# Partial sums of y added up in DRAM by accumulating transfers instead of on the vector engine

## The chip, the cores and the metric

One core of a Trainium2 chip runs the kernel. The metric is the device time of one execution in microseconds (us). Five engines work side by side, each with its own instruction stream: TensorE (PE, matrix products; PEld is its weight load), VectorE (DVE), ScalarE (ACT), GpSimd (POOL) and SyncE (SP). Transfers between DRAM and the on-chip memory SBUF are issued by an engine's stream and carried by 16 DMA engines that all streams share. PE writes only to PSUM, eight banks of 128 x 512 floats.

## What is computed

```
x = retention(q, k, v)                 # 4 x 576 = 2304 tokens, 512 wide
h = x @ w_in;  g = h * tanh(softplus(h));  x2 = g @ w_out      # first layer, d_ff 2048
h = max(x2 @ w_in2, 0);  out = (h * h) @ w_out2                # second layer, d_ff 2048
```

The retention part takes the first 63 us of the span and is not touched by the change's text. All matrices of the two layers are split into a high and a low part (fp32r), and each product is made of three matmuls.

## The kernel before

**Staging.** Tokens are cut into three blocks of SB = 768 (index v). The 2048 inner columns are cut into four quarters (index p, a pass). A *visit* u is one (layer m, pass p, block v), in the order m, p, v: 24 visits, numbered 0 to 23, of some 31 us each. Visits 0 to 11 are the first layer, visits 12 to 23 the second. Each visit has two half-visits, `fp` 0 and 1; each makes seven products (P1 to P7, a Strassen-like scheme on the block, L735) from the seven tiles `ring` (the split x of the block) and the weights `win`.

**The second product.** `y_group` (L812) multiplies the activated g with `wout` and collects y in four PSUM tiles `py`, over the four f of a visit. The y of visit u is made partly in visit u and finished in visit u+1: in the first layer, token half th = 0 is finished by y03 and th = 1 by y13, at the end of the first half-visit; in the second layer both are finished at the end of the visit's second half (names `y00` to `y13` in the lists `first_half`, `second_half`, `run`).

**Adding up.** y of the first quarter (p = 0) is copied by ACT from `py` into the tile `part[v]` (SBUF). y of quarters 1 to 3 is added onto it by DVE (L836). After the last quarter, `part` of the first layer is x of the second: `sums_x` and `split_x` form the seven sums and split them into `ring`. In the second layer the last quarter's sum is stored to `out` by SP, 19 transfers (the last block of 128 tokens in two halves of 256 columns).

**x again.** ring of a block is kept in DRAM (`keep`, tile `d`) at its first visit and fetched (`fetch`, seven transfers of 768 KB) for each later one, into the same seven tiles as PE frees them. For visit 3 alone x is loaded unsplit from the DRAM copy `raws` and split again (`again_x`).

**Order.** A class `Plan` records every operation with a cost, works out due times backwards from PE's fixed order, and then lists the operations per engine by due time. So an operation that is added or taken away can move others, far from where it stands; the order on each engine and on SP's and POOL's queues is then fixed, and each stream waits in order. The lines that the change and the prediction touch: `dma` (L288, SP's transfers), `y_group` (L812, L836), `again_x` and `load`, `scale_v` (L494 on ACT, L496 on POOL and DVE), `update` (the state copies `sbd`, L274 is the common ACT helper).

```
            if p == 0:
                act(dst, y, n=n, reads=[("py", o)], writes=kd)
            else:
                dve(
                    lambda dst=dst, y=y: nc.vector.tensor_tensor(dst, y(), dst, op=ALU.add),
                    n, [("py", o)] + kd, kd,
                )
```

Of the kernel before, what the change touches and what calls it, by code (L numbers as in the profile page):

```python
# [8 lines left out]
F32 = mybir.dt.float32  # L9
# [3 lines left out]
ALU = mybir.AluOpType  # L13
# [6 lines left out]
DM = H * D  # L20
DFF = 2048
P = 128
KD = DM // P
# [6 lines left out]
NPASS = NF // FPP  # L30
TH = 384
SB = 2 * TH
NSB = NT // SB
# [2 lines left out]
GS = 12  # L36
ES = 4
CPS = 4
WARM = 8
OUT_SLOTS = 6  # L40
PAD = 96
# [18 lines left out]
SLACK = 3.0  # L60
# [167 lines left out]
def kernel(  # L228
# [25 lines left out]
    cst = space("cst", **att_kw)  # L254


    part = tiles_of(act_p, NSB, [P, KD, SB], F32, "part")
    part2 = [t.rearrange("p k n -> p (k n)").rearrange("p (t e) -> p t e", e=DM) for t in part]
# [7 lines left out]
    py = tiles_of(ps_p, 4, [P, DM], F32, "py")  # L266
    t2 = act_p.tile([P, 2, TH], F32, tag="t2", name="t2")
    t3 = act_p.tile([P, 2, TH], F32, tag="t3", name="t3")

    plan = Plan()  # L270
    late = {}

    def act(out, in_, func=AF.Copy, n=512, reads=(), writes=(), **kw):
        fn = lambda: nc.scalar.activation(out() if callable(out) else out, in_() if callable(in_) else in_, func, **kw)  # L274
        plan.add("ACT", 0.09 + n * 0.00084, fn, reads, writes)

    def dve(fn, n, reads, writes):
        plan.add("DVE", 0.07 + n * 0.00104, fn, reads, writes)
# [8 lines left out]
    def dma(out, in_, reads, writes, size, early=0.0, slack=0.0, by=1e9, eng=None, cost=0.45):  # L287
        fn = lambda: (eng or nc.sync).dma_start(out=out, in_=in_)  # L288
        plan.add("SP", cost, fn, reads, writes, size / 0.40e6, early=early, slack=slack, by=by)

    def minus(eng, out, a, b):
        return lambda: eng.tensor_tensor(out, a, b.bitcast(F32), op=ALU.subtract)  # L292
# [38 lines left out]
    def split_in(gp):  # L331
# [26 lines left out]
            cut(2, slice(2, 4), yb, kb, 512)  # L358
        return lambda: cut(2, slice(2, 3), a21, kb, 256)

    raws = [dram_p.tile([P, 2, TH], F32, tag=f"raw{i}", name="xraw") for i in range(4)]
# [5 lines left out]
    def load(dst, i, kd, early=0.0):  # L367
        dma(dst, raws[i], [("raws", i)], [kd], P * 8 * TH, early=early)

    def first_x(i):  # L370
        b, ks = blocks_of(0)
        cut_x(i, b[(0, 1, 3, 2)[i]], ks[(0, 1, 3, 2)[i]])

    def again_x(name):
        i = X_AT[name]
        lo = [r[:, 1].bitcast(F32) for r in ring]
        kl = [("x", i, 1) for i in range(7)]
        tt = nc.vector.tensor_tensor
        t1 = sums.rearrange("p a n -> p (a n)").rearrange("p (k n) -> p k n", k=2)
        k1 = [("s", j) for j in range(3)]  # L380
        if name == "P1":
            load(t2, 0, "t2", 10.0)
        if name in ("P1", "P2", "P3"):
            load(lo[i], i if i < 2 else 3, kl[i], 4.0)
            cut_x(i, lo[i], kl[i])
        elif name == "P6":
            load(lo[4], 3, kl[4], 4.0)
        elif name == "P5":
            load(lo[3], 2, kl[3], 4.0)
            dve(lambda: tt(t3, lo[4], lo[3], op=ALU.subtract), 768, [kl[4], kl[3]], ["t3"])  # L390
            dve(lambda: tt(t1, lo[3], t2, op=ALU.subtract), 768, [kl[3], "t2"], k1)
            dve(lambda: tt(t2, lo[4], t1, op=ALU.subtract), 768, [kl[4], *k1], ["t2"])
            cut_x(4, t2, "t2")
            cut_x(3, t1, *k1)
        elif name == "P7":
            cut_x(5, t3, "t3")
        elif name == "P4":
            load(lo[6], 1, kl[6], 4.0)
# [260 lines left out]
    done_with += [("cp", j) for j in range(CPS)] + [("e", j) for j in range(ES)]  # L659
    plan.loose.add(plan.add("PE", 0.0, open_late, (), done_with))  # L660

    visits = [(m, p, v) for m in range(2) for p in range(NPASS) for v in range(NSB)]
    nv = len(visits)
    count = dict(g=0, e=0, ac=0, py=0, cp=0, direct=0)
    gs = {}

    def take(what, n):
        count[what] += 1
        return (count[what] - 1) % n
# [118 lines left out]
    def y_group(u, th, f):  # L788
        m, p, v = visits[u]
        g = m * NF + p * FPP + f  # L790
        j = gs.pop((u, th, f))
        kw = ("wo", g % OUT_SLOTS)
        na = KD if m == 0 else TH // P
        last = (u, th) == (nv - 1, 1)
        if f == 0:
            yb[0] = [take("py", 4) for _ in range(na + last)]
            yc = [slice(0, DM)] * na
            if last:
                yc[-1:] = [slice(0, DM // 2), slice(DM // 2, DM)]
            yb[1] = yc  # L800
        for i, (o, cols) in enumerate(zip(*(yb[k] for k in range(2)))):
            ky = ("py", o)

            def mm(i=min(i, na - 1), o=o, cols=cols):
                s = slice(i * P, i * P + P)
                y, gt, wo = py[o], late["g"][j], late["wout"][g % OUT_SLOTS]
                if m == 0:
                    y, st, mv = y[:, :TH], wo[:, :, s], gt
                else:
                    y, st, mv = y[:, cols], gt[:, :, s], wo[:, :, cols]  # L810
                for k, (a, b) in enumerate(((1, 0), (0, 1), (0, 0))):
                    nc.tensor.matmul(  # L812
                        y, st[:, a], mv[:, b],
                        start=(f == 0 and k == 0), stop=(f == FPP - 1 and k == 2),
                        skip_group_check=True,
                    )

            plan.add("PE", 0.52 if m == 0 else 0.694 * (cols.stop - cols.start) / DM, mm, [kw + (0,), kw + (1,), ("g", j, 0), ("g", j, 1), ky], [ky])
        if f < FPP - 1:
            return  # L820
        for i, (o, cols) in enumerate(zip(yb[0], yb[1])):
            i = min(i, na - 1)
            if m == 0:
                dst, n = part[v][:, i, TH * th : TH * th + TH], TH
                kd = [("part", v, i // 2, th)]
            else:
                dst, n = part2[v][:, 3 * th + i, cols], cols.stop - cols.start
                kd = [("p2", v, 3 * th + i, cols.start)]
                if p == 0:
                    kd += [("part", v, k, t) for k in range(2) for t in range(2)]  # L830
            y = lambda o=o, c=slice(0, TH) if m == 0 else cols: py[o][:, c]
            if p == 0:
                act(dst, y, n=n, reads=[("py", o)], writes=kd)
            else:
                dve(
                    lambda dst=dst, y=y: nc.vector.tensor_tensor(dst, y(), dst, op=ALU.add),  # L836
                    n, [("py", o)] + kd, kd,
                )
            if m == 1 and p == NPASS - 1:
                r = SB * v + TH * th + P * i  # L840
                dma(out[r : r + P, cols], dst, kd, [("out", r, cols.start)], P * 4 * n)

    first_half = "P1 P2 y03 P6 P5 y10 P7 y11 P4 y12 P3 y13".split()
    second_half = "P1 P2 y00 P6 P5 P7 y01 P4 y02 P3".split()
# [153 lines left out]
```

## Time and profile before

| | |
|---|---|
| time, median of 3 runs | 819.7 us (819.58 to 819.82) |
| the profiled execution's own time | 819.48 us |
| its span, first to last instruction | 817.7 us |
| PE busy | 810.6 us, 99% |
| DVE / ACT / POOL busy | 577.5 / 446.2 / 11.5 us |
| DMA traffic | 188.78 MB, 62.0% of the 16 engines' time |
| granted TensorE clock | 1.000 |

The profile gives busy time per engine, the chain of work that ended last (followed back from the last instruction), waits by releaser, and the transfers with the time from issue to landing. PE's busy time is that of pipelined matmuls; where they follow each other without a gap, PE sets the pace.

### The profile page before, as it was taken

The numbers are of one execution on the slowest core, as the hardware profiler recorded it, in microseconds if no ns is written. First come the engines' busy times: TensorE is split into PE (matmuls) and PEld (weight loads), VectorE is DVE, ScalarE is ACT, GpSimd is POOL, SyncE is SP. The second block draws the span as 40 slices with busy tenths as digits, with TensorE's granted clock in tenths as the row PEclk, the third lists the DMA queues.
The fourth block names the chain that finished last, engine by engine and source line by source line (L and its number), as shares of the span: only waits on it lengthen the run. The fifth ranks groups of instructions, "written<-read, shape, count | busy, mean of one in ns | idle before, by whom it ended". The sixth has DMA issues, their size and how long they took to land.

```text
span 817.7 us, 13326 instructions
## 1 busy us (share of the span) xinstructions
PE 810.6 (99%) x5216; PEld 770.3 (94%) x5216; DVE 577.5 (71%) x1096; ACT 446.2 (55%) x916; POOL 11.5 (1%) x20
## 2 busy tenths in 40 slices
PE   9999999999999999999999999999999999999998
PEld 7899999999999999999999898898898898898996
DVE  5899997987488636785489984995479844743443
ACT  2697586753455335553377675763465553652541
POOL 3200000000000000000000000000000000000000
PEclk9999999999999999999999999999999999999999
DMA  9985865984675754763844844963756843735812
GB/s 342 405 307 183 319 262 201 387 304 173 246 249 190 282 203 128 313 224 152 290 174 177 322 179 168 346 235 140 270 186 218 343 155 116 270 135 213 303 44 78
DMA packets 44158, 188.78 MB, mean 231 GB/s; under 512 B 4928, under 2 KB 6848, under 8 KB 44096
## 3 DMA queue, kind: packets, MB, share of 16 engines
q1 hardware_dynamic: 44096, 187.93, 62.0%
q8 instruction: 41, 0.67, 0.3%
q14 instruction: 21, 0.17, 0.1%
HBM read 148.59 MB, written 39.32 MB: 230 GB/s over the span
## 4 chain that ended last, share of the span: by engine, by line
PE 95%; DMA 4%; ACT 0%; DVE 0%; SPq 0%; issue 0%; DVEq 0%; ACTq 0%
PE py L812 48%; PE h L735 41%; PE h L773 2%; DMA qk<-in_qk_dram 1%; PE h L517 1%; DMA kv<-in_v_t_dram 1%; PE py L571 1%; DMA kv<-in_kv_dram 1%; PE py L535 1%; PE py L549 1%; DVE part L836 0%; ACT sbd L274 0%; ACT kv L494 0%; SPq L288 0%; DVEq L993 0%
## 5 line engine op out<-in xcount | busy, mean ns | idle before, releaser
L735 PE MATMUL h<-ring,win 128*128 128x384 f32 x1932 | 354.5, 334 | 0.0
L735 PEld LDWEIGHTS h<-ring,win 128*128 128x128 f32 x1932 | 337.5, 188 | 1.9
L812 PE MATMUL py<-g,wout 128*128 128x384 f32 x1152 | 214.6, 334 | 0.0
L812 PE MATMUL py<-wout,g 128*128 128x512 f32 x876 | 201.3, 387 | 0.0
L812 PEld LDWEIGHTS py<-g,wout 128*128 128x128 f32 x1152 | 201.0, 188 | 0.0
L812 PEld LDWEIGHTS py<-wout,g 128*128 128x128 f32 x876 | 162.4, 188 | 32.7 <-DVE g L292 0.2
L274 ACT ACTIVATE cp<-h 128x384 f32<-128x384 f32 x138 | 67.6, 490 | 150.4 <-PE h L735 149.7
L836 DVE TENSOR_TENSOR part<-py,part 128x384 f32<-128x384 f32 (+2 forms) x127 | 74.5, 607 | 41.0 <-PE py L812 40.7
L718 DVE TENSOR_TENSOR h<-h,cp 128x384 f32<-128x384 f32 x92 | 51.8, 563 | 67.7 <-PE h L735 64.6
L292 DVE TENSOR_TENSOR g<-e,g 128x384 fp32r<-128x384 f32 x118 | 64.5, 554 | 36.6 <-ACT g L274 36.3
L274 ACT ACTIVATE h<-h 128x384 f32<-128x384 f32 x74 | 35.3, 477 | 60.8 <-DVE h L718 42.1
L274 ACT ACTIVATE g<-e 128x384 fp32r<-128x384 f32 x118 | 60.6, 523 | 3.8 <-DVE e L689 1.7
L292 DVE TENSOR_TENSOR g<-h,g 128x384 fp32r<-128x384 f32 x74 | 40.7, 551 | 22.5 <-ACT g L274 22.5
L274 ACT ACTIVATE e<-h 128x384 f32<-128x384 f32 x72 | 34.1, 488 | 31.4 <-PE h L735 20.4
L718 DVE TENSOR_TENSOR e<-h,cp 128x384 f32<-128x384 f32 x46 | 25.5, 553 | 29.5 <-ACT cp L274 29.4
L321 DVE SCALAR_TENSOR_TENSOR y<-raw,y 128x512 uint32<-128x512 uint32 x64 | 43.9, 685 | 3.3 <-ACT y L274 3.2
L274 ACT ACTIVATE y<-raw 128x512 f32<-128x512 uint32 x64 | 42.8, 668 | 5.7 <-DVE win L285 2.2
L322 DVE CUSTOM_DVE_ANT_0 y<-z,y 128x1024 uint16<-128x1024 uint16 x64 | 43.5, 685 | 0.4
L274 ACT ACTIVATE g<-h 128x384 fp32r<-128x384 f32 x74 | 36.2, 490 | 1.3
L274 ACT ACTIVATE wout<-y 128x512 fp32r<-128x512 f32 x32 | 20.1, 631 | 29.4 <-PE py L812 23.1
L274 ACT ACTIVATE e<-e 128x384 f32<-128x384 f32 x46 | 24.1, 523 | 18.5 <-DVE e L718 18.2
L687 ACT ACTIVATE e<-e 128x384 f32<-128x384 f32 x60 | 31.5, 526 | 1.8
(61 smaller groups left out, 585.0 us busy)
## 6 DMA issues: line engine op xcount, KB each, us to landing
ring<-d SPq DMA_DIRECT2D x119, 768.0 KB, 6.6
raw<-in_wp_dram SPq DMA_DIRECT2D x64, 512.0 KB, 4.6
d<-ring SPq DMA_DIRECT2D x42, 768.0 KB, 4.8
qk<-in_qk_dram SPq DMA_DIRECT2D x16, 512.0 KB, 8.7
kv<-in_kv_dram SPq DMA_DIRECT2D x12, 512.0 KB, 9.8
out_dram<-part SPq DMA_DIRECT2D x17, 256.0 KB, 2.1
ring<-xraw SPq DMA_DIRECT2D x6, 384.0 KB, 4.9
kv<-in_kv_dram SPq DMA_DIRECT2D x8, 256.0 KB, 6.0
```

The costliest lines, as they stand in the source:

```text
L274: fn = lambda: nc.scalar.activation(out() if callable(out) else out, in_() if callable(in_) else in_, func, **kw)
L292: return lambda: eng.tensor_tensor(out, a, b.bitcast(F32), op=ALU.subtract)
L321: dve(lambda: stt(yu, hi, 0x80000000, yu, op0=band, op1=bor), 512, kr + [ky], [ky])
L322: dve(lambda: nc.vector.tensor_tensor(yu, z, yu, op=ALU.add), 512, [kz, ky], [ky])
L517: nc.tensor.matmul(psc[2 * x0 + e][to, hp, :n], t[r, 1, hp], t[r, 0, hp], start=True, stop=True)
L535: nc.tensor.matmul(pso[o][half(e), hp, : t.shape[3]], sbd[:, x, hp, e], t[:, 0, hp], start=(hp == 0), stop=False, skip_group_check=True,)
L687: eng.activation(e(), e(), AF.Square)
L718: lambda: nc.vector.tensor_tensor(dst(), bank(b)(), late["cp"][j], op=ALU.add),
L735: nc.tensor.matmul(dst(), w[:, hw, wi, s], ring[i][:, hx, k], start=(new and k == 0 and n == 0), stop=(k == 1 and n == 2), skip_group_chec ...
L773: nc.tensor.matmul(dst(), w[:, hw, wi, s], ring[i][:, hx, a], start=(k == a == n == 0), stop=(k == a == 1 and n == 2), skip_group_check=True,)
L812: nc.tensor.matmul(y, st[:, a], mv[:, b], start=(f == 0 and k == 0), stop=(f == FPP - 1 and k == 2), skip_group_check=True,)
L836: lambda dst=dst, y=y: nc.vector.tensor_tensor(dst, y(), dst, op=ALU.add),
```

## The change

y of the first quarter is still copied by ACT; in the first layer into `part`, and from there stored by SP into a DRAM tile `sums_d[v][i]`. y of every later quarter is copied by ACT into one of four staging tiles `st`, and GpSimd issues a transfer that adds the tile onto the DRAM tile. In the second layer all quarters go through `st` and directly onto `out`: a store by SP for p = 0, then three accumulating transfers. x of the second layer is loaded from `sums_d` by `again_x`, in place of `sums_x` and `split_x`. `part` is given up after visit 3 and its room holds `st`. The diff, cut:

```
+STS = 4
...
+    early = ExitStack()
+    part = tiles_of(space("part", stack=early), NSB, [P, KD, SB], F32, "part")
...
+    def add_up(out, in_, first, reads, writes, size):
+        if first:
+            fn = lambda: nc.sync.dma_start(out=out, in_=in_())
+        else:
+            fn = lambda: nc.gpsimd.dma_start(out=out, in_=in_(), accum_op=ALU.add)
+        plan.add("SP", 0.45, fn, reads, writes, size / 0.40e6, slack=0.0 if first else SLACK)
...
+    def load(dst, m, v, i, kd, early=0.0):
+        src, ks = (sums_d[v][i], ("sum", v, i)) if m else (raws[i], ("raws", i))
+        dma(dst, src, [ks], [kd], P * 8 * TH, early=early)
...
+            elif m == 0:
+                if i % 2 == 0:
+                    l = take("st", STS)
+                kd = ("st", l)
+                dst = lambda l=l, i=i: late["st"][l].rearrange("p (a n) -> p a n", a=2)[:, i % 2]
+                src = lambda l=l: late["st"][l].rearrange("p (a n) -> p a n", a=2)
+            else:
+                l = take("st", STS)
+                kd = ("st", l)
+                dst = src = lambda l=l, n=cols.stop - cols.start: late["st"][l][:, :n]
+            n = c.stop - c.start
+            act(dst, y, n=n, reads=[("py", o)], writes=[kd])
             if m == 0:
-                dst, n = part[v][:, i, TH * th : TH * th + TH], TH
-                kd = [("part", v, i // 2, th)]
+                if i % 2:
+                    q = 2 * th + i // 2
+                    add_up(sums_d[v][q], src, p == 0, [kd], [("sum", v, q)], P * 8 * TH)
             else:
...
-                dve(
-                    lambda dst=dst, y=y: nc.vector.tensor_tensor(dst, y(), dst, op=ALU.add),
-                    n, [("py", o)] + kd, kd,
-                )
-            if m == 1 and p == NPASS - 1:
                 r = SB * v + TH * th + P * i
-                dma(out[r : r + P, cols], dst, kd, [("out", r, cols.start)], P * 4 * n)
+                add_up(out[r : r + P, cols], src, p == 0, [kd], ..., P * 4 * n)
...
+        if u == NSB + 1:
+            hand_over()
...
-        if nxt and nxt[1] == 0:
+        if nxt and nxt[:2] == (0, 0):
             sums_x(nxt[2])
...
-                            if u + 1 == NSB:
-                                again_x(name)
+                            if u + 1 == NSB or m and not p:
+                                again_x(name, m, v)
```

Where it moves instructions, at the end of the program. DVE, the last rows before:

```order
L292 TENSOR_TENSOR g<-e,g 128x384
L718 TENSOR_TENSOR h<-h,cp 128x384
L292 TENSOR_TENSOR g<-e,g 128x384 x2
L836 TENSOR_TENSOR part<-py,part 128x512 x5
L836 TENSOR_TENSOR part<-py,part 128x256 x2
L993 UNCONDITIONAL_BRANCH
```

ACT's last rows now:

```order
L275 ACTIVATE e<-h 128x384
L705 ACTIVATE e<-e 128x384
L275 ACTIVATE g<-e 128x384
L275 ACTIVATE st<-py 128x512 x5
L275 ACTIVATE st<-py 128x256 x2
L1019 UNCONDITIONAL_BRANCH
```

and POOL's rows from its last computation in the retention part on, where before only the branch followed:

```order
L506 TENSOR_TENSOR kv<-kv,vdec_sb 128x256 x8
L296 DMA xsum<-st 128x768 x36
L296 DMA out_dram<-st 128x512 x53
L296 DMA out_dram<-st 128x256 x2
L1019 UNCONDITIONAL_BRANCH
```

The seven last adds of DVE have become copies of ACT, and their stores, which stood on SP, are the last of 91 transfers on POOL.

SP's queue near the start, in the retention part (`raw` are packed weights of the first layer; `in_v_t` and `in_qk_t` are the 64 tokens at the end of each sequence), before:

```order
L288 DMA kv<-in_kv_dram 128x1024
L288 DMA raw<-in_wp_dram 128x1024
L288 DMA kv<-in_kv_dram 128x1024
L288 DMA raw<-in_wp_dram 128x1024
L288 DMA qk<-in_qk_t_dram 128x512
L288 DMA kv<-in_v_t_dram 128x512
L288 DMA qk<-in_qk_t_dram 128x512
L288 DMA kv<-in_kv_dram 128x1024
L288 DMA qk<-in_qk_dram 128x1024
```

and now:

```order
L289 DMA kv<-in_kv_dram 128x1024 x2
L289 DMA qk<-in_qk_t_dram 128x512
L289 DMA kv<-in_v_t_dram 128x512
L289 DMA qk<-in_qk_t_dram 128x512
L289 DMA raw<-in_wp_dram 128x1024
L289 DMA kv<-in_kv_dram 128x1024
L289 DMA qk<-in_qk_dram 128x1024
L289 DMA kv<-in_kv_dram 128x1024
L289 DMA raw<-in_wp_dram 128x1024
```

The first two weight loads, which stood ahead of the tail's three loads, now stand behind them. ACT's rows at the same place (`kv<-kv,vdec_sb` scales v, four instructions of 64 columns for each half of a chunk; `sbd` is the state that PE reads next), before:

```order
L274 ACTIVATE ring<-part 128x768 x2
L274 ACTIVATE y<-raw 128x512
L494 ACTIVATE kv<-kv,vdec_sb 128x64 x4
L274 ACTIVATE sbd<-py 64x8x64 x2
L494 ACTIVATE kv<-kv,vdec_sb 128x64 x20
```

and now:

```order
L275 ACTIVATE ring<-part 128x768 x2
L504 ACTIVATE kv<-kv,vdec_sb 128x64 x8
L275 ACTIVATE sbd<-py 64x8x64 x2
L504 ACTIVATE kv<-kv,vdec_sb 128x64 x8
L275 ACTIVATE y<-raw 128x512
```

Both halves of the tail's v are now scaled ahead of the two state copies, and the first weight conversion stands behind them.

## Rows read from the trace of the kernel before

**Rows 1.** The page: busy time, share of the span and instructions by engine.

```profile
PE 810.6 (99%) x5216; PEld 770.3 (94%) x5216; DVE 577.5 (71%) x1096; ACT 446.2 (55%) x916; POOL 11.5 (1%) x20
```

**Rows 2.** Waits of PE, whole span: us in total, times, longest.

```profile
PE py L591 <- DVE ring L589: 1.5, 1, 1.5
PE py L535 <- ACT sbd L274: 1.1, 2, 0.8
```

**Rows 3.** The chain that ended last, end of the span: start, us, what.

```profile
801.24 11.11 PE py L812 x57
...
812.37 1.71 DVE part L836 x3
```

**Rows 4.** Timelines of PE and SP, end of the span: start, us, what.

```profile
811.24 2.50 PE L812 MATMUL py<-wout,g 128*128 128x256 f32 x14
...
813.09 2.01 SPq L288 DMA_DIRECT2D out_dram<-part  x4
```

**Rows 5.** DMA issues, whole span: count, KB each, median us from issue to landing.

```profile
ring<-d SPq DMA_DIRECT2D x119, 768.0 KB, 6.6
...
t<-xraw SPq DMA_DIRECT2D x1, 384.0 KB, 3.6
...
out_dram<-part SPq DMA_DIRECT2D x2, 128.0 KB, 2.0
```

**Rows 6.** Groups of instructions by form: count | busy, mean ns | idle before.

```profile
L274 ACT ACTIVATE part<-py 128x384 f32<-128x384 f32 x24 | 11.1, 492 | 2.0 <-PE py L812 1.9
L274 ACT ACTIVATE part<-py 128x512 f32<-128x512 f32 x18 | 10.7, 598 | 13.8 <-PE py L812 13.0
...
L836 DVE TENSOR_TENSOR part<-py,part 128x384 f32<-128x384 f32 x72 | 37.8, 550 | 0.2
...
L617 POOL TENSOR_TENSOR qdec_sb<-qdec_sb,qstep 128x512 f32<-128x512 f32 x3 | 3.3, 1109 | 3.0 <-DMA qdec_sb<-in_qdec_dram 3.0
L617 POOL TENSOR_TENSOR qdec_sb<-qdec_sb,qstep 128x256 f32<-128x256 f32 x1 | 0.6, 616 | 0.0
```

**Rows 7.** Instructions of the tiles xraw and raw: ns min/median/max, first and last.

```profile
L288 SPq DMA_DIRECT2D xraw<-part x4: 568/768/1265, 60.3 to 62.6; - x4
...
L318 DVE TENSOR_SCALAR z<-raw x64: 409/418/429, 29.9 to 652.0; 128x512 uint32<-128x512 uint32 x64
```

**Rows 8.** The chain that ended last, retention part: start, us, what.

```profile
21.68 9.22 DMA kv<-in_v_t_dram
...
31.23 0.82 ACT kv L494 x3
32.07 0.60 ACT sbd L274
32.69 0.60 ACT sbd L274
```

**Rows 9.** Timelines of SP and PE, retention part: start, us, what.

```profile
16.49 0.33 SPq L288 DMA_DIRECT2D raw<-in_wp_dram  x1
...
19.04 0.33 SPq L288 DMA_DIRECT2D raw<-in_wp_dram  x1
...
30.01 1.92 PE L571 MATMUL py<-a,kv 128*64 128x128 f32 x32
```

**Rows 10.** Stretches: PE, PEld, DVE, ACT, POOL busy; clock, DMA share, GB/s.

```profile
20.00:40.00 20.00, 18.93 (x414) 17.63 (x412) 16.63 (x30) 12.39 (x35) 4.74 (x8) 1.00 1.03 405
...
97.00:128.00 31.00, 31.00 (x181) 31.00 (x180) 27.56 (x52) 21.32 (x42) 0.00 (x0) 1.00 0.70 260
...
252.00:283.00 31.00, 31.00 (x181) 31.00 (x180) 25.06 (x53) 15.46 (x30) 0.00 (x0) 1.00 0.68 245
```

**Rows 11.** Ring loads between visits 3 and 4: SP's and PE's timelines.

```profile
178.07 3.44 SPq L288 DMA_DIRECT2D ring<-d  x2
...
192.44 1.20 PE L735 MATMUL h<-ring,win 128*128 128x384 f32 x6
```

**Rows 12.** DMA issues at 178 to 180 us: count, KB, us to landing.

```profile
ring<-d SPq DMA_DIRECT2D x1, 768.0 KB, 9.5
```

More of the change, by code (lines that the diff above doesn't have):

```diff
@@ L254 @@
     cst = space("cst", **att_kw)
-    part = tiles_of(act_p, NSB, [P, KD, SB], F32, "part")
-    part2 = [t.rearrange("p k n -> p (k n)").rearrange("p (t e) -> p t e", e=DM) for t in part]
+    early = ExitStack()
+    part = tiles_of(space("part", stack=early), NSB, [P, KD, SB], F32, "part")
     ring = tiles_of(act_p, 7, [P, 2, 2, TH], F32R, "ring")
@@ L285, in pair, with dma @@
         dve(lambda: nc.vector.tensor_tensor(get(out), a, get(b).bitcast(F32), op=op), n, reads, writes)
-    def dma(out, in_, reads, writes, size, early=0.0, slack=0.0, by=1e9, eng=None, cost=0.45):
-        fn = lambda: (eng or nc.sync).dma_start(out=out, in_=in_)
+    def dma(out, in_, reads, writes, size, early=0.0, slack=0.0, by=1e9, cost=0.45):
+        fn = lambda: nc.sync.dma_start(out=out, in_=in_)
         plan.add("SP", cost, fn, reads, writes, size / 0.40e6, early=early, slack=slack, by=by)
+    def add_up(out, in_, first, reads, writes, size):
[4 more added lines that the diff above has]
+        plan.add("SP", 0.45, fn, reads, writes, size / 0.40e6, slack=0.0 if first else SLACK)
     def minus(eng, out, a, b):
@@ L359, in split_in @@
         return lambda: cut(2, slice(2, 3), a21, kb, 256)
+    sums_d = [[dram_p.tile([P, 2, TH], F32, tag=f"sum{v}_{i}", name="xsum") for i in range(4)] for v in range(NSB)]
     raws = [dram_p.tile([P, 2, TH], F32, tag=f"raw{i}", name="xraw") for i in range(4)]
@@ L365, in save @@
             dma(raws[i], b, [k, ("step", *LAST)], [("raws", i)], P * 8 * TH)
-    def load(dst, i, kd, early=0.0):
-        dma(dst, raws[i], [("raws", i)], [kd], P * 8 * TH, early=early)
+    def load(dst, m, v, i, kd, early=0.0):
+        src, ks = (sums_d[v][i], ("sum", v, i)) if m else (raws[i], ("raws", i))
+        dma(dst, src, [ks], [kd], P * 8 * TH, early=early)
     def first_x(i):
@@ L372, in first_x, with again_x @@
         cut_x(i, b[(0, 1, 3, 2)[i]], ks[(0, 1, 3, 2)[i]])
-    def again_x(name):
+    def again_x(name, m, v):
         i = X_AT[name]
@@ L381, in again_x @@
         if name == "P1":
-            load(t2, 0, "t2", 10.0)
+            load(t2, m, v, 0, "t2", 10.0)
         if name in ("P1", "P2", "P3"):
-            load(lo[i], i if i < 2 else 3, kl[i], 4.0)
+            load(lo[i], m, v, i if i < 2 else 3, kl[i], 4.0)
             cut_x(i, lo[i], kl[i])
         elif name == "P6":
-            load(lo[4], 3, kl[4], 4.0)
+            load(lo[4], m, v, 3, kl[4], 4.0)
         elif name == "P5":
-            load(lo[3], 2, kl[3], 4.0)
+            load(lo[3], m, v, 2, kl[3], 4.0)
             dve(lambda: tt(t3, lo[4], lo[3], op=ALU.subtract), 768, [kl[4], kl[3]], ["t3"])
@@ L397, in again_x @@
         elif name == "P4":
-            load(lo[6], 1, kl[6], 4.0)
+            load(lo[6], m, v, 1, kl[6], 4.0)
             dve(lambda: tt(t2, lo[6], t2, op=ALU.subtract), 768, [kl[6], "t2"], ["t2"])
@@ L660, with open_more, hand_over @@
     plan.loose.add(plan.add("PE", 0.0, open_late, (), done_with))
+    def open_more():
+        early.close()
+        late["st"] = tiles_of(space("more"), STS, [P, 2 * TH], F32, "st")
+    def hand_over():
+        was = [("part", v, k, t) for v in range(NSB) for k in range(2) for t in range(2)]
+        plan.loose.add(plan.add("PE", 0.0, open_more, (), was + [("st", j) for j in range(STS)]))
     visits = [(m, p, v) for m in range(2) for p in range(NPASS) for v in range(NSB)]
     nv = len(visits)
-    count = dict(g=0, e=0, ac=0, py=0, cp=0, direct=0)
+    count = dict(st=0, g=0, e=0, ac=0, py=0, cp=0, direct=0)
     gs = {}
@@ L822, in y_group @@
             i = min(i, na - 1)
+            c = slice(0, TH) if m == 0 else cols
+            y = lambda o=o, c=c: py[o][:, c]
+            if m == 0 and p == 0:
+                kd = ("part", v, i // 2, th)
+                dst = part[v][:, i, TH * th : TH * th + TH]
+                src = lambda k=i // 2: part[v][:, 2 * k : 2 * k + 2, TH * th : TH * th + TH]
+            elif m == 0:
[10 more added lines that the diff above has]
+            act(dst, y, n=n, reads=[("py", o)], writes=[kd])
             if m == 0:
-                dst, n = part[v][:, i, TH * th : TH * th + TH], TH
-                kd = [("part", v, i // 2, th)]
-            else:
[L827 to L834, printed above, removed]
-                dve(
-                    lambda dst=dst, y=y: nc.vector.tensor_tensor(dst, y(), dst, op=ALU.add),
-                    n, [("py", o)] + kd, kd,
-                )
-            if m == 1 and p == NPASS - 1:
+                if i % 2:
+                    q = 2 * th + i // 2
+                    add_up(sums_d[v][q], src, p == 0, [kd], [("sum", v, q)], P * 8 * TH)
+            else:
                 r = SB * v + TH * th + P * i
-                dma(out[r : r + P, cols], dst, kd, [("out", r, cols.start)], P * 4 * n)
+                add_up(out[r : r + P, cols], src, p == 0, [kd], [("out", r, h) for h in range(cols.start // 256, cols.stop // 256)], P * 4 * n)
     first_half = "P1 P2 y03 P6 P5 y10 P7 y11 P4 y12 P3 y13".split()
```

## The prediction
> **What bounds the kernel now.** I read the busy shares first: PE is busy for 99% of the span, DVE for 71%, ACT for 55%, POOL for 1% [rows 1]. Then PE's waits, to see whether anything can give PE time back: one wait of 1.5 us at the very start and 1.1 us, in two pieces, for the state copies `sbd` in the retention part are nearly all of it, and none lies after that part [rows 2]. From 33 to 812 us PE's matmuls follow each other without a gap. So work that DVE loses is worth nothing by itself. The time can change in three places only: in the 1.1 us near the start, in what follows PE's last matmul, and where the change makes PE wait for the first time. A difference of 0.2%, 1.64 us here, is about what a measurement of this kernel can tell from no change.
>
> **The end.** Before, DVE takes the last four sums as PE finishes them, from 812.37 us on [rows 3]; SP issues their four stores between 813.09 and 815.10 us, the last one beginning at 815.10 - 0.33 = 814.77, and PE itself ends at 811.24 + 2.50 = 813.74 [rows 4]. A store of 128 KB lands 2.0 us after its issue [rows 5], at 816.77, and the span ends 0.93 us behind that.
>
> Now ACT copies. A copy of 512 columns takes it 0.60 us, one of 384 columns 0.49 [rows 6]; at that slope, an estimate, 256 columns take 0.39. The copies end at 812.97, 813.57, 813.96 and 814.35: no later than DVE's adds. The difference is in the transfers, which POOL issues one after another. The trace has no transfer of POOL and none that accumulates, so both prices are bounded.
> - *Issue on POOL.* Below: as on SP, 0.33 us. Above: the slowest issue on SP, 1.27 us [rows 7]. I take what POOL needs for an instruction on tiles of these sizes, as the nearest rows of that engine: 1.11 us for 512 columns, 0.62 for 256 [rows 6]. First issue at 813.0, the next at 814.1, 815.2, the last at 815.84.
> - *Landing.* Below: a plain store, 2.0 us. Above: a load from DRAM (3.6 us on a quiet queue) and then the store, 5.6 us [rows 5], since the old sum must be read before the new one is written. I take the middle, 3.8, as the read may overlap the staging of the other operand.
>
> Sum: 815.84 + 3.8 + 0.93 = 820.57, that is **+2.9 us**. With both lower ends it is 814.35 + 2.0 + 0.93 = 817.28, or -0.4; with both upper ends 813.0 + 3 x 1.27 + 5.6 + 0.93 = 823.34, or +5.6.
>
> A store that lands in 2.0 us on an empty queue is what the trace shows for SP [rows 5]. The Trainium skill ("DMA: Bandwidth & Descriptors", Anatomy of one DMA) gives for a transfer issued by GpSimd some 2.0 us plus bytes over 436 GB/s, nothing extra being said of accumulation; by it 128 KB would take 2.3 us and the end would grow by 1.4 us instead of 2.9. No row here shows such a transfer.
>
> **The start.** The change's text does not touch the retention part, but the order of SP's queue moves: two weight loads, issued at 16.49 and 19.04 us ahead of the tail's v, now stand behind it [rows 9]. In that stretch the DMA engines are full, 405 GB/s at a share of 1.03 [rows 10], so 2 x 512 KB are 2.6 us. The tail's v, issued at 21.68, landed 9.22 us later at 30.90 and released ACT's scaling (three of its four instructions took 0.82 us), then the two `sbd` copies of 0.60 us each until 33.29 [rows 8]. Now it lands at about 28.3. ACT scales both halves first, eight instructions in some 2.1 us, until 30.4, then copies `sbd` until 31.6, before PE's previous block ends at 30.01 + 1.92 = 31.93 [rows 9]. The wait of 1.1 us goes: **-1.07 us**. Bounds: -1.07 (PE waits for nothing else there) and 0. The weights come later by as much; their first product starts at 63 us and they were converted by some 46, so 17 us cover it. Without that cover each microsecond of delay would be one of PE.
>
> **What is added in between.** All of it lies beside PE if it is in time.
> - *ACT's copies* in place of 127 adds of DVE: 0.49 us each against 0.55 at 384 columns [rows 6]. `py` comes free no later. In the visits of the first quarter ACT does these copies already, and PE runs through 97 to 128 us without a gap [rows 10]. ACT's stream gets 4 x 0.49 = 2 us more per token half, and the new waits of ACT, for a free `st`, hold up the activations behind them and through these PE. In the first layer a slot comes back after a visit, 31 us; in the second the first two of three are wanted again 8 us later, when th = 1 follows th = 0. By the upper ends the second of three is back after 2 x 1.27 + 5.6 = 8.1 us, just in time; by the values taken, after 2 x 1.11 + 3.8 = 6.0. So I cost this at nothing.
> - *Traffic.* A visit of the first layer adds up 4 x 384 KB. At 405 GB/s a plain transfer of that takes 0.97 us of the DMA engines. Below: 1 x, 3.9 us per visit. Above: 4 x, 15.5 us (source read, old sum read, sum written, and as much again for the turn-around). The middle stretches have a DMA share of 0.68, so 31 x 0.32 = 9.9 us free [rows 10]. I take 2 x, 7.8 us, read and write of the old sum being the longer side: it fits.
> - *Ring loads beside them* (PE waits for these first). The tightest I find is the last but one of the seven loads between visits 3 and 4: issued at 178.07, it lands 9.5 us later, at 187.6, and PE takes it at 192.44 [rows 11, 12]: 4.9 us to spare. The usual landing is 6.6 us [rows 5]. One pair of accumulating transfers falls in the burst of seven loads, by 2 x a delay of 3.9 us at most: covered.
> - *SP's queue.* The loads of the second layer's x wait for the last accumulation of their block, made a visit earlier (31 us), and the first stands ahead of seven ring loads; it is late only if an accumulation takes over 8 us. Their splits on ACT and DVE are as many as from `part`, and visit 3 was fed in this way without a wait of PE [rows 2].
>
> **Sum.** +2.9 - 1.07 = +1.8 us on the profiled execution's 819.48, which lies 0.2 below the median: 821.3, against the median **821.5 us**, slower by 0.22%.
>
> **The rivals.**
> - *The end hardly grows* (chance 0.32). POOL's issues cost little and overlap the landing of the one before. It decides if the four issues take under 0.6 us each and the landing under 3 us. For it: nothing else is on POOL or in the DMA queues then. Against it: POOL's own instructions of that size take 1.1 us. Time: between 819.7 - 0.4 - 1.07 = 818.2 and 820.9, say 819.9: no change, or just faster. The skill's figure above falls in this case, at 820.0.
> - *Ring loads come late in the first layer* (0.13). At 4 x, the pair in the burst costs 7.8 us, 2.9 more than the 4.9 to spare, in the tightest of eight visits, less in the looser ones (6.6 us landing instead of 9.5 leaves as much as is lacking). At half of 2.9 in each it is +11 us: 832. For it: the DMA engines are full during these bursts. Against it: the mean share of 0.68.
> - *POOL's descriptors come late* (0.05). Some of DVE's instructions may shut POOL out. DVE's shift and mask instructions at 0.42 us for 512 columns run at a faster pace than its adds [rows 7]; nothing here shows POOL stopped by them. The Trainium skill ("SBUF — State Buffer", SBUF: two separate sides) says that while DVE runs an instruction in a two-port mode GpSimd cannot write descriptors, and gives 0.62 us for a transfer alone and 3.1 us beside it. As a mechanism here: should three issues take over 8 us in the second layer, ACT waits for `st` up to 2 us at the end of each of 12 visits, and PE for ACT in part of them: 819.7 + 1.8 + some 6 = 828. At the end of the kernel DVE has no work left, so the tail would not show it.
>
> **Chances.** The forecast itself, an end of +1.9 to +5.6 with the start gained or not, 0.50: of it 0.08 stay under 1.64 us. The end that hardly grows, 0.32: 0.29 no change, 0.03 faster. Both late cases are slower. Together: faster 0.03, no change 0.37, slower 0.60. The forecast's own range is 820.5 to 825.3 (819.7 + 5.6 with nothing won at the start). To hold 8 in 10 the range goes down into the first rival, to 819.2, and up a little into the late ones, to 826.5.
>
> **What would show it.** Right: PE's matmuls without a gap from the retention part to the last y; no wait of PE for `sbd` near 32 us; four transfers of POOL after the last copy, over 0.5 us apart, the last landing over 3 us after its issue; the span's end some 6 to 7 us behind PE's last matmul instead of 4.0. Wrong: PE waiting for a ring load or for ACT in visits 4 to 23, the wait for `sbd` still there, or a tail as long as before.

## The result and the profile after

The changed kernel takes **830.5 us** (median of 4 runs, 829.48 to 832.8), the kernel before beside it 819.7 (819.58 to 819.82): a ratio of 1.0131, 95% interval 1.0119 to 1.0144. The prediction said 821.5 us and at most 826.5. The direction was right, the size was not: 10.8 us lost instead of 1.8.

The profiled execution's span is 828.6 us, 10.9 longer than before. The page of the changed kernel, busy time and DMA queues, answers to [rows 1]:

```profile
PE 812.0 (98%) x5216; PEld 771.1 (93%) x5216; DVE 511.6 (62%) x963; ACT 504.9 (61%) x1049; POOL 92.5 (11%) x111
...
q1 hardware_dynamic: 50240, 200.91, 63.9%
q0 software_dynamic: 13104, 28.32, 21.2%
```

DVE lost 66 us of work and PE won nothing by it. The queue of POOL's transfers, q0, moves 12% of the bytes and takes a quarter of the DMA engines' busy time.

**Where the 10.9 us are.** The waits of PE in the changed kernel (us in total, times, longest) answer to [rows 2]:

```profile
PE py L830 <- DVE g L300: 2.2, 1, 2.2
PE py L601 <- DVE ring L599: 1.5, 1, 1.5
PE py L581 <- POOL kv L506: 1.2, 1, 1.2
PE py L559 <- issue: 0.2, 1, 0.2
```

The wait for `sbd` is gone. The wait for POOL's `kv`, near 8 us, is longer than in the kernel before, where it was

```profile
PE py L571 <- POOL kv L496: 0.5, 1, 0.5
```

And there is one wait that was not there before: 2.2 us for DVE's `g`, under the second layer's products with `wout`. The chain that ended last shows its place (start, us, what), the change from the first to the second layer. Before:

```profile
448.44 4.16 PE h L735 x24
...
484.72 4.12 PE py L812 x18
```

After:

```profile
447.39 2.96 PE h L753 x17
450.37 8.57 DMA ring<-xsum
...
458.96 0.06 DVE sums L401
...
460.70 0.55 DVE g L300
...
462.60 0.47 DVE g L300
...
463.11 12.09 PE py L830 x45
475.20 12.70 PE h L753 x72
487.90 4.12 PE py L830 x18
```

At the first of these places PE is 1.05 us ahead of the kernel before (447.39 against 448.44), at the last 3.18 us behind (487.90 against 484.72). So the stretch between, 36.28 us before, now takes 40.51: **the change of layers costs 4.2 us**. From there to PE's end only another 0.2 is lost.

What happens in it: this is visit 12, the first of the second layer, and SP loads x of visit 13 from `xsum`. One of these loads takes 8.57 us to land, and it is not issued before 450.37, when the products end whose ring half it fills (447.39 + 2.96). The waits of DVE and of ACT between 445 and 475 us show who stands still for it:

```profile
DVE sums L401 <- DMA ring<-xsum: 2.2, 1, 2.2
```

```profile
ACT ring L275 <- DMA ring<-xsum: 2.3, 2, 2.0
```

DVE's queue is in order: behind the subtraction that waits for x (L401, at 458.96) stand the low parts of visit 12's own `g` (L300, at 460.70 and 462.60), which PE needs for y. So PE waits, though nothing that it multiplies then depends on the x that is late. The windows of the changed kernel around it (PE, PEld, DVE, ACT, POOL busy; granted clock, DMA share, GB/s):

```profile
440.00:450.00 10.00, 10.00 (x59) 10.00 (x58) 9.05 (x18) 8.56 (x19) 1.72 (x2) 1.00 1.04 347
450.00:460.00 10.00, 10.00 (x51) 9.02 (x51) 6.07 (x13) 6.64 (x13) 0.00 (x0) 1.00 1.05 310
...
463.10:466.00 2.90, 2.89 (x7) 2.28 (x8) 2.90 (x5) 2.28 (x5) 0.00 (x0) 0.55 1.02 422
...
464.00:466.00 2.00, 2.00 (x6) 1.58 (x5) 2.00 (x4) 1.41 (x3) 0.00 (x0) 0.50 1.01 418
466.00:468.00 2.00, 2.00 (x8) 1.60 (x7) 1.94 (x3) 1.83 (x4) 0.00 (x0) 0.81 1.04 428
```

The same first window of the kernel before:

```profile
440.00:450.00 10.00, 10.00 (x59) 10.00 (x58) 9.45 (x21) 7.64 (x16) 0.00 (x0) 1.00 0.32 102
```

Two things are to be read here. The DMA engines, at a share of 0.32 before in the first window, are full. And after PE's 2.2 us of standing still the granted clock is 0.50, the lower level of 1.2 GHz, from 464 to 466 us; over the first 2.9 us it is 0.55 and over the next two 0.81, which is 2.9 x 0.45 + 2 x 0.19 = 1.7 us of PE's time. The wait and the clock are 3.9 of the 4.2 us.

**The end.** PE ends at 817.12 us, 11.5 before the span does; before it was 4.0. POOL's transfers in the changed kernel's timeline (the row of all four, and that of the last one alone), which answer to SP's stores in [rows 4]:

```profile
816.65 3.53 POOL L296 DMA_DIRECT2D out_dram<-st  x4 [5.68 <-ACT st L275]
...
818.47 1.71 POOL L296 DMA_DIRECT2D out_dram<-st  x1
```

The landing of the last two, against 2.0 us in [rows 5], and SP's last wait, before and now:

```profile
out_dram<-st POOLq DMA_DIRECT2D x2, 128.0 KB, 5.5
```

```profile
SPq L993 <- PEq L993: 0.6, 2, 0.4
```

```profile
SPq L1019 <- PEq L1019: 4.1, 2, 3.6
```

The last transfer begins 1.35 us after PE's end (SP's last store 1.03 before): +0.3. It lands at 818.47 + 5.5 = 823.97: +3.5. And from there to the end of the span it is 4.6 us instead of 0.93: **+3.7**. In that last piece no engine works and no byte moves; SP stands at the barrier with which the program ends. The whole: -1.05 + 4.2 + 0.2 + 7.5 = 10.9 us. The three parts of the 7.5 follow the terms of the prediction; experiment 4 shows that the landing is not what the end waits for.

### The profile page after: what moved, and what is told of

It reads as the page before. It is cut to its first block, busy times and chain, and to the rows that moved or that the text cites. A ratio compares the mean times of both kernels' runs of the same rounds, so it can differ in the third digit from the quotient of the medians.

```text
span 828.6 us, 13673 instructions
## 1 busy us (share of the span) xinstructions
PE 812.0 (98%) x5216; PEld 771.1 (93%) x5216; DVE 511.6 (62%) x963; ACT 504.9 (61%) x1049; POOL 92.5 (11%) x111
## 3 DMA queue, kind: packets, MB, share of 16 engines
q0 software_dynamic: 13104, 28.32, 21.2%
## 4 chain that ended last, share of the span: by engine, by line
PE 95%; DMA 2%; issue 1%; POOL 1%; DVE 0%; SPq 0%; POOLq 0%; ACT 0%
PE py L830 46%; PE h L753 40%; PE h L791 2%; PE py L581 2%; PE h L527 2%; PE py L545 2%; DMA ring<-xsum 1%; PE py L559 1%; DMA vdec_sb<-in_vdec_dram 1%; POOL out_dram L296 1%; SPq L289 0%; DVE g L300 0%; POOLq L1019 0%; DVE t L402 0%; POOL kv L506 0%
## 5 line engine op out<-in xcount | busy, mean ns | idle before, releaser
L275 ACT ACTIVATE st<-py 128x384 f32<-128x384 f32 (+2 forms) x145 | 76.2, 544 | 77.7 <-PE py L830 73.8
L300 DVE TENSOR_TENSOR g<-e,g 128x384 fp32r<-128x384 f32 x118 | 64.6, 554 | 43.1 <-ACT g L275 42.6
L296 POOL DMA_DIRECT2D out_dram<-st x55 | 48.9, 1109 | 321.3 <-ACT st L275 321.3
L296 POOL DMA_DIRECT2D xsum<-st x36 | 31.4, 889 | 389.1 <-ACT st L275 234.1
L300 DVE TENSOR_TENSOR g<-h,g 128x384 fp32r<-128x384 f32 x74 | 40.9, 553 | 35.3 <-ACT g L275 34.7
L705 ACT ACTIVATE e<-e 128x384 f32<-128x384 f32 x66 | 34.6, 525 | 1.9
```

The costliest lines, as they stand in the source:

```text
L296: fn = lambda: nc.gpsimd.dma_start(out=out, in_=in_(), accum_op=ALU.add)
L705: eng.activation(e(), e(), AF.Square)
```

## The experiments

Three questions: which half of the change makes which loss; whether it is the adding, the transfers by POOL or the loads of x; and what the late end of the program hangs on.

**1. The second layer alone.** The first layer is left as before; y of the second goes through four staging pieces and is added up on `out`.

```
-                dve(lambda: tensor_tensor(dst, y(), dst, op=ALU.add), ...)      # m == 1
+            act(dst, y, n=n, reads=[("py", o)], writes=kd)
+            fn = lambda: nc.gpsimd.dma_start(out=to, in_=dst, accum_op=ALU.add)
```

> Only the second layer is changed: its y goes through four staging tiles (pieces of the first block's part) and is added up on out by GpSimd's transfers; the first layer is summed by DVE in SBUF and split from there, as before. Theory (three separate places: the turn of the layers costs 4.4 us through the first layer's sums in DRAM, the end costs 7.5 us): no wait of PE at the turn, the last matmul within 0.3 us of before's 813.7, the span ends 11 to 12 us behind it, 827.2 us. Rival (the turn's stall comes from the second layer's staging and stores): the stall of 2 us stays and the time is 831.

Measured: 825.9 us, ratio 1.0069 (1.0054 to 1.0084). There is no wait at the change of layers (448.12 to 484.40, 36.28 us as before), PE ends at 813.6, and the tail is 10.1 us. SP's last wait:

```profile
SPq L1000 <- PEq L1000: 2.3, 2, 1.9
```

So the second layer's transfers alone make most of the long end, 6.1 us of the 7.5 (10.1 against 4.0 before); with the first layer's in the program it is 1.4 us longer, though none of those is issued after 450 us.

**2. The first layer alone.** The sums of the first layer are made in DRAM and x is loaded from there; the second layer as before.

```
             elif m == 0:
+                act(st[:, i % 2], y, n=n, reads=[("py", o)], writes=[kd])
...
             else:
+                dve(lambda: nc.vector.tensor_tensor(dst, y(), dst, op=ALU.add), n, [("py", o)] + kd, kd)
```

> Only the first layer is changed: its sums are made in DRAM by GpSimd's transfers and x of the second layer is loaded from there; the second layer is summed by DVE in SBUF and stored by SP, as before. Theory: the stall at the turn stays (2 us of waiting and some 1.7 us at the lower clock, PE some 4.4 us late), the last store lands as before, but the program ends 3.7 us later because POOL has issued transfers at all: 827.8 us. Rival (the late end belongs to the accumulating transfers at the end): 824.1. Rival (the stall needs the second layer's traffic too): 823.4 with the late end, 819.7 without.

Measured: 823.3 us, ratio 1.0041 (1.0026 to 1.0056). The stall is there, and the tail is that of the kernel before, 4.0 us. Chain and SP's last wait of this kernel:

```profile
448.54 1.94 PE h L745 x12
450.48 8.85 DMA ring<-xsum
...
487.66 4.12 PE py L822 x18
```

```profile
SPq L1020 <- PEq L1020: 0.6, 2, 0.5
```

39.1 us for the stretch, 2.8 lost, not 4.2. The wait is as long as in the changed kernel (2.2 us for `g`, here behind ACT's queue, which waits for the same kind of load), but in this execution the granted clock stays at 1.00 behind it. The four executions agree with a price of some 1.7 us for the low clock: the two with a mean granted clock of 1.000 took 822.3 and 822.6 us, the two with 0.997 took 824.0 and 824.4. That 36 accumulating transfers, the last at 450 us, don't make the end late was the rival's case: the late end needs transfers near the end.

**3. One plain transfer by POOL.** The kernel before, with one load of 384 KB, at some 113 us, issued by POOL.

```
-            load(t2, 0, "t2", 10.0)
+            load(t2, 0, "t2", 10.0, nc.gpsimd)
```

> The kernel before with one single plain load (384 KB, at some 113 us) issued by POOL instead of SP. Theory (any transfer issued by POOL makes the program's end 3.7 us longer): 823.4 us, the last matmul and the last landing as before. Rival (the late end comes from many transfers, or from accumulating ones, or from those close to the end): 819.7 us.

Measured: 820.0 us, ratio 1.0002 (0.9993 to 1.0012). That any transfer of POOL makes the end longer is false: this one, early in the program, does not.

**4. Stores in place of additions.** The changed kernel with plain transfers of the same bytes.

```
-            fn = lambda: nc.gpsimd.dma_start(out=out, in_=in_(), accum_op=ALU.add)
+            fn = lambda: nc.gpsimd.dma_start(out=out, in_=in_())
```

> The changed kernel with every accumulating transfer of POOL turned into a plain store to the same place; it leaves out the additions of the partial sums, so only the last quarter's share is in the output. Theory (adding is what makes the transfers slow: they take the DMA engines 2.4 times as long and land in 5.5 us instead of 2): the last transfers land 2 to 2.5 us after their issue, the stall at the turn is gone or below 1 us, the late end of 3.7 us stays, the gain of 1.07 us at the start stays: 823 to 824 us. Rival (the landing of 5.5 us is that of POOL's issue, not of the adding): landing 5 us or more at the end, 826.5. Rival (the turn's stall comes from the loads of x and the copies kept, not from the adding): PE waits 2 us at the turn as in the changed kernel, 827.5.

Measured: 825.2 us, ratio 1.0066 (1.0049 to 1.0082). Its DMA queue of POOL's transfers over the whole span, landings, and SP's last wait:

```profile
q0 software_dynamic: 7216, 28.32, 9.1%
```

```profile
xsum<-st POOLq DMA_DIRECT2D x36, 384.0 KB, 5.0
...
out_dram<-st POOLq DMA_DIRECT2D x2, 128.0 KB, 2.4
```

```profile
SPq L1019 <- PEq L1019: 6.1, 2, 5.6
```

The same 28.32 MB take 9.1% of the DMA engines' time as stores (74.9 us of 823.0) and 21.2% as additions (175.7 of 828.6): adding costs 2.3 times as much. Between 445 and 456 us, POOL's queue and the four loads of `xsum` in the changed kernel:

```profile
q0 software_dynamic: 226, 0.65, 30.2%
...
ring<-xsum SPq DMA_DIRECT2D x4, 384.0 KB, 8.1
```

and without the adding:

```profile
q0 software_dynamic: 160, 0.79, 19.6%
...
ring<-xsum SPq DMA_DIRECT2D x4, 384.0 KB, 5.7
```

The stretch takes 36.4 us, PE does not wait in it, and at the end 128 KB land in 2.4 us. So the stall and the long landing come from the adding. The late program end does not: it is there in full, 6.4 us behind the last landing (814.15 + 2.4). And the landing hardly counts: it is 3.1 us shorter, the tail behind PE's end only 1.3 us (10.2 against 11.5), and of these 1.2 are POOL's, whose last issue ends 1.9 us behind PE in place of 3.1.

**5. SP's order at the start alone.** The kernel before, with later due times for the first two weight loads.

```
-RAW_BY = {0: -6.0, 1: -3.0, 2: 1.0, 3: 4.0}
+RAW_BY = {0: -1.0, 1: 0.0, 2: 1.0, 3: 4.0}
```

> The kernel before with one change: the due times of the first two weight loads are later (-1 and 0 us in place of -6 and -3), so that SP issues them behind the tail's v, as in the changed kernel. Theory (the gain of 1.07 us at the start comes from this order of SP's queue alone): the first product of visit 0 at 62.3 instead of 63.34 us, no later wait of PE, 819.7 - 1.07 = 818.6 us. Rival (it needs the changed kernel's other order behind it, or is taken back by weights that come late): 819.7 us.

Measured: 818.9 us, ratio 0.9989 (0.998 to 0.9998): the fastest of all kernels here, if barely. PE's waits:

```profile
PE h L517 <- DMA qk<-in_qk_dram: 1.5, 2, 0.9
PE py L591 <- DVE ring L589: 1.4, 1, 1.4
PE py L571 <- POOL kv L496: 0.7, 1, 0.7
```

The wait for `sbd` goes, as theory had it, but PE's order in the retention part shifts too and meets a new wait for `qk`. The first product of visit 0 comes at 61.12 us, earlier than the 62.3 of the theory, but at the change of layers PE is 0.24 us ahead (448.20), not 1.07. So moving the weights behind the tail's v takes the old wait away; what takes its place depends on the order around it, and the lead of 1.05 us is seen in the changed kernel's order, not in this one.

**6, 7, 8. How many transfers, and when.** The kernel before, where DVE still adds and POOL stores plainly. In e6 POOL issues the last four stores, in e11 the last seven, in e10 the last four and 52 weight loads before them.

```
+                dma(out[...], dst, kd, ..., eng=nc.gpsimd if last else None)            # e6, e10
+                dma(out[...], dst, kd, ..., eng=nc.gpsimd if u == nv - 1 else None)     # e11
+        dma(r..., src, after, kr, ..., eng=nc.gpsimd if i >= 12 else None)              # e10
```

> The kernel before, with its last four stores issued by POOL as plain transfers; DVE still adds. Theory (a program ends late when POOL has issued transfers shortly before the end, however few): PE's end as before, at 813.7; the stores land 2.4 us after their issue at some 817.5; then 5 to 6.5 us to the end of the span in place of 0.93, so 825 us. Rival (the late end needs many transfers of POOL in one program, 79 to 127 as in the kernels that showed it): the span ends about 1 us behind the last landing, 820.4 us.

> The kernel before, with its last seven stores (both token halves of the last visit) issued by POOL as plain transfers, as many in the last 15 us as in the changed kernel, and none before. Theory (the number over the whole program makes the late end): as e6, 821.3 us. Rival (the number of POOL's transfers in the last 15 us makes it): the end 7 us or more behind POOL's last issue, 825 us.

> As e6_last_four_by_pool (the kernel before, its last four stores issued by POOL), and 52 of the 64 weight loads issued by POOL too, so that 52 transfers of POOL lie behind the last four. Theory (the late program end grows with the number of transfers that POOL has issued in the program): the end comes 7 us or more behind POOL's last issue, against some 3 in e6, and the time is some 4 us over e6's 821.25, 825 us. Rival (it depends on what POOL issued in the last microseconds alone): 821.3 us.

(The numbers of transfers named for e6 are miscounted: the kernels that showed a late end had 55 and 91.) Measured: e6 821.25 us, ratio 1.0017 (1.0008 to 1.0026); e11 821.0, 1.0014 (1.0005 to 1.0023); e10 824.0, 1.0047 (1.0033 to 1.006). SP's last wait in e6 (word for word the same in e11) and, below, in e10:

```profile
SPq L993 <- PEq L993: 0.6, 2, 0.5
```

```profile
SPq L993 <- PEq L993: 2.4, 2, 2.0
```

In e10 PE ends 0.6 us later than in e6 (814.88 against 814.24), and the rest of the 2.7 us is the end. Put together with the other kernels (times in us; "issue" is the end of POOL's last issue, read from POOL's timeline, and a landing is the last transfer's start with the median of the last transfers):

| kernel | POOL's transfers | issue to span end | landing to span end |
|---|---|---|---|
| e6, e11 | 4, 7 | 3.1, 3.2 | 1.2, 1.4 |
| experiment 1 | 55, adding | 7.0 | 3.1 |
| e10 | 56 | 5.4 | 3.5 |
| changed kernel, experiment 10 | 91, adding | 8.4, 8.6 | 4.6, 4.6 |
| experiment 4 | 91 | 8.3 | 6.4 |

With 91 transfers the end comes 8.3 to 8.6 us behind POOL's last issue, whether they add or not and whether they landed early or late. With 4 or 7 it comes little more than 1 us behind the landing. That the end grows with the number is borne out; the theory's figure for e10 (7 us or more) was too high. What POOL does in that time no row shows. One rival is not tested: after PE's last matmul the granted clock falls to 0.50 and stays there to the end, for 6.8 us in the changed kernel, 7.2 in experiment 4, 6.5 in experiment 1 and 2.3 in e10. It does not make the late end by itself, since in e6 and e11 it is 0.50 for the last 2.4 and 1.7 us and the end is not late; whether it lengthens it, no run here shows.

**9. The last third of the tokens summed on chip.** The changed kernel, but block v = 2 of the second layer summed by DVE in a tile `p2` and stored by SP. POOL's last transfer begins at 788.9 us.

```
+            elif v == 2:
+                dst = lambda: late["p2"][:, 3 * th + i, cols]
+                act(dst, y, ...) if p == 0 else dve(tensor_tensor(dst(), y(), dst(), op=ALU.add), ...)
```

> The changed kernel, with the last third of the tokens (v = 2) of the second layer summed by DVE in SBUF as before, and stored by SP; the other two thirds are still added up in DRAM, so that POOL's last transfer is issued some 30 us before the end. Theory (landing and late program end both come from POOL's transfers right at the end): the stall at the change of layers stays, PE ends near 817.1, the span 4.0 us later as in the kernel before, 821.1, and the time is 830.5 - 7.5 = 823.0 us. Rival (the late program end comes with the number of POOL's transfers): 3.7 us more, 826.7 us.

Measured: 824.6 us, ratio 1.0058 (1.0044 to 1.0071). The span ends 4.2 us behind PE's last matmul, as the theory had it; the 1.6 us over its 823.0 lie ahead of the change of layers, which PE reaches at 449.31 instead of 447.39, since the planner gave the retention part another order. SP's last wait:

```profile
SPq L1033 <- PEq L1033: 0.9, 2, 0.7
```

72 transfers of POOL, the last issue over 33 us before the end, cost the end next to nothing (4.2 us behind PE against 4.0).

**10. x loaded early.** The changed kernel, with x of the second layer loaded into four tiles `sx` of its own, four loads a block instead of seven, and no ring half to wait for.

```
-            load(lo[i], m, v, i if i < 2 else 3, kl[i], 4.0)
+            plan.add("SP", 0.45, fn, [("sum", v, i)], [("sx", i)], ..., early=10.0, slack=SLACK)
```

> The changed kernel, with x of the second layer loaded once into four tiles of its own, up to a visit half ahead of its use, in place of seven loads into ring halves that come free late. Theory (the stall at the change of layers is the late landing of these loads, on which DVE's and ACT's queues stand still, with the low clock behind it): no wait of PE there, DVE waits for no such load, PE ends near 813.1, and the time is 830.5 - 4.0 = 826.5 us. Rival (the accumulating transfers fill the DMA engines and something else, a ring load or the weights, is late in its place): PE still waits between 436 and 470 us, 829 to 830.5 us.

Measured: 828.2 us, ratio 1.0103 (1.0089 to 1.0117). Chain, and ACT's waits between 455 and 480 us:

```profile
464.89 10.09 DMA out_dram<-st
476.12 10.69 PE h L781 x60
486.81 4.12 PE py L858 x18
```

```profile
ACT st L275 <- DMA out_dram<-st: 2.7, 1, 2.7
```

The wait for x is gone and the stretch takes 37.5 us (449.33 to 486.81), 3.0 less than in the changed kernel. But the rival is right in part: the next wait stands behind it. One of the first block's plain stores lands in 10.09 us in the still full DMA engines, a slot of `st` is not back, ACT's queue stands, and PE waits 0.9 us for a copy. The start is 1.9 us later here as well.

**11. The three remedies together.** Experiments 9 (e7 in the text below) and 10 (e8), and the first block's opening copies staged in `p2`, which is free then. The due times of the first two weight loads are moved as well, to -4 and -1.

```
-            elif v == 2:
+            elif v == 2 or (v, p) == (0, 0):
```

> The changed kernel with three edits together: the last third of the tokens of the second layer summed in SBUF and stored by SP (as in e7_last_block_on_chip), x of the second layer loaded once and early (as in e8_x_loaded_early), and the first third's opening stores staged in the then free slots of that sum instead of the four common ones; the first two weight loads' due times -4 and -1 us. Theory (the loss over the kernel before is three things and no more: the landing and the late program end, 7.5 us together, and the stall at the change of layers, 4.2 us): 830.5 - 7.5 - 4.2 = 818.8 us, or up to 820.7 if the retention part comes out 1.9 us longer by its new order, as it did in e7 and e8; PE waits nowhere after 70 us, and the span ends 4.0 us behind PE. Rival (the added traffic of 41 MB costs PE time in some other place as soon as these are gone): 822 us or more.

Measured: 819.9 us, ratio 0.9999 (0.999 to 1.0008). All of PE's waits of 0.2 us or more:

```profile
PE py L627 <- DVE ring L625: 1.5, 1, 1.5
PE py L607 <- POOL kv L532: 0.2, 1, 0.2
PE py L607 <- DVE a L561: 0.2, 1, 0.2
PE py L859 <- DVE wout L286: 0.2, 1, 0.2
```

The stretch takes 36.25 us (448.69 to 484.94), as before, and the 10.8 us are back, with two thirds of the second layer and all of the first still added up in DRAM. So the three places hold the change's costs to within 1 us: the span still ends 4.6 us behind PE, 0.6 more than before. It is not faster than the kernel before: the lead of 1.05 us at the start is not in this order (448.69 against 448.44 before), and DVE's freed time is worth nothing to PE.

## Why the prediction was wrong

- **The start**, -1.07: -1.05 at 447 us. The mechanism is right, the wait for `sbd` is gone; that the number fits so closely is partly luck. PE comes to the place 0.54 us later than before (its block begins at 30.55 against 30.01), having waited 1.2 us for `kv` and not 0.5; the kernel of experiment 4, with the same order here, waited 0.5 and leads by 1.30 at the change of layers (447.14). From there to the next product PE takes 2.8 us in place of 4.4 (until 33.34 against 34.41), a gain of 1.6. And the order of the two weight loads is not the whole of it (experiment 5).
- **ACT's copies, and the ring loads of the first layer**, nothing: right. PE carries its lead of the start to 447 us (1.07 at its first product of visit 0, 1.05 there). The traffic, taken as 2 x a plain transfer, is 2.3 x. The rivals of late ring loads and of descriptors held up by DVE did not happen; POOL's slowest issue is 1.71 us, the last of all, when DVE has no work left. That the end hardly grows did not happen either.
- **"SP's queue"**, nothing: the first step that failed, 4.2 us. The prediction made x late "only if an accumulation takes over 8 us", so it looked for a sum that is not ready. Accumulations did take over 8 us (8.3 at the median of the 36), but the sums were ready all the same: visit 13's were issued by 418.5 us, and its late load at 450.37. What was late was the load itself, in DMA engines that the adding keeps full (8.1 us against 5.7 with plain stores, experiment 4), and into ring halves that PE must free first; taking away either one removes this wait (experiments 4 and 10). Visit 3, taken as evidence, was fed beside less traffic (its loads landed in 4.9 us at the median, at a DMA share of 0.74 from 137 to 150 us). And the cover was looked for at PE's products of x, not at what stands behind the waiting subtraction on DVE: the `g` of the running visit. What counts there is what an operation in DVE's queue waits for, not how much work DVE has. The lower clock then added 1.7 us to the 2.2 of the wait.
- **"Issue on POOL"**, 0.62 to 1.11 us one after another: the mean of 1109 ns for `out` meets the 1.11 by luck, as the rows it was taken from are of another kind of work. The last four take 0.86 and 1.01 us for 512 columns, 1.36 and 1.71 for 256, and they do not stand one after another: they start 0.54 to 0.74 us apart while earlier ones still run, so the last one begins 1.35 us after PE's end and not 2.10.
- **"Landing"**, 3.8 taken of 2.0 to 5.6: the second step that failed, mis-sized: 5.5 us measured, at the upper end. The middle had no row for it. The Trainium skill ("DMA: Bandwidth & Descriptors", Anatomy of one DMA) gives, as an estimate from its fit, 2.3 us for 128 KB by GpSimd; the plain transfers of experiment 4, with 2.4, agree with it, and the accumulating ones do not fall under it.
- **"The span ends 0.93 us behind that"**: the third step that failed, 3.7 us. It was carried over from a kernel whose POOL issues no transfer, with no bound, though POOL's transfers were the unknown of the whole sum. The range had no room for it: with 5.6 for the landing and the upper issue the end was to grow by 5.6 us at most, and it grew by 7.5. And the path was wrong, not only the size: the end does not follow the last landing but comes 8.3 to 8.6 us behind POOL's last issue with 91 transfers, at a landing of 2.4 us as at 5.5 (experiment 4). So the right landing alone would not have given the right end. What the end waits for stays open.

## What to carry to other kernels

When work moves from an engine to transfers, cost three things apart from the traffic: what stands behind each instruction that will wait for a load, on its own in-order queue; the landing of the last transfers when nothing covers them; and the program's own end, which here ran behind POOL's last issue and hid the landing. Have the last outputs issued on the queue after which the program ends soonest (here SP's), and give a load that is made from such sums a tile that is free early. And a DVE that is busy for 71% beside a PE busy for 99% is no reason to move its work: with the losses removed, the time was that of the kernel before.

## What the runs showed of the hardware

- An accumulating transfer takes 2.3 times the DMA engines' time of a plain store of the same bytes (21.2% against 9.1% of the span for 28.32 MB), in 13104 packets instead of 7216, and POOL needs 0.85 us or more to issue one, 0.54 for a plain one.
- POOL's transfers overlap on POOL: four issues of 0.86 to 1.71 us took 3.53 us together.
- The program's end comes later with the number of transfers that POOL has issued, if the last of them is near the end: 3.1 and 3.2 us behind the last issue at 4 and 7, 8.3 to 8.6 at 91. Where the last is over 33 us before the end, 72 cost next to nothing. What it waits for stays open, and that it is proportional to the number is not shown: 55 and 56 gave 7.0 and 5.4 us.
- The granted clock behind one stall of PE of 2.2 us: 0.50 from 464 to 466 us in the changed kernel, worth 1.7 us in all; 1.00 throughout in the profiled execution of experiment 2, with a stall as long.
